# Linear attention with an adapter mixture on one core: epsilon added on VectorE in 16 of 36 steps, logits placed behind the sums of k and v, one batch's sums spread over three steps

## The chip, the core and the metric

The kernel runs on one core of a Trainium2 chip. Its engines each work through their own list of instructions in order: PE (TensorE: matrix products, with PEld for the load of the stationary operand), DVE (VectorE), ACT (ScalarE), POOL (GpSimd) and SP, which here only issues stores. They wait for each other through semaphores. Matrix products land in PSUM, a small memory of eight banks per partition, from where DVE or ACT must move them to SBUF before the bank can be used again. The metric is the device time of one execution in microseconds (us); lower is better.

## What is computed

q, k and v have 8 batches, 8 heads, 576 positions and 64 features. First comes a linear attention whose weights are cos and sin of the position, then a mixture of small adapters over the 4608 rows of 512 features that the attention gives.

```python
r = np.maximum(x, 0.0)
phi(x) = np.concatenate([r * cos_w, r * sin_w], axis=-1)      # for q and for k
kv  = np.einsum('bhsf,bhsd->bhfd', k_p, v)
z   = np.sum(k_p, axis=2)
num = np.einsum('bhsf,bhfd->bhsd', q_p, kv)
den = np.einsum('bhsf,bhf->bhs', q_p, z)[..., None] + 1e-06
x   = num / den
...
logits = x @ w_gate                   # 8 experts, the best 2 are kept
w = softmax of the two kept logits
out = x + sum over the two of w * ((x @ A[e]) @ B[e])
```

The `1e-06` in `den` is the epsilon that the change is about.

## The kernel before

**Tiles.** The 4608 rows are 36 tiles of 128 rows, numbered n from 0 to 35; two batches make nine tiles, of which the middle one (n = 4, 13, 22, 31, called mixed) takes half of its rows from each. The loop `for n in range(NT - 1)` does one tile in each step. The order on every engine is the order in which the program text issues the instructions; no scheduler moves them.

**One step n, in its order.** `evac_x(n-1)` (DVE) copies the transposed x of the tile before from the bank `xz` to `xT`. `normalise(n)` (DVE) takes the reciprocal of the denominators and multiplies, which gives `xt`. `move_q(n+1)` transposes and scales the next tile's q on PE (line 213, from tile 27 on line 201) into two `qd` banks, and ACT moves both to SBUF with the ReLU (line 229). Then come the `logits` of `early_at` (PE, line 300, four products for a tile into the bank `za`), the sums `kv` of `kv_at` (PE, line 180, eight products for one position s, accumulated in the banks `cd`), `gate_a` and `gate_b` of a group of three tiles (DVE, small operations and `zg`), one or two output tiles (`emit`: `delta_x` and `delta_z` on PE into a `qd` bank, or a `cd` bank where the step has no sums, then `evac_o` on ACT and a store), `transp_x(n)` (PE, line 274) and `transp_z` (PE, line 348) of a finished group into `xz`, the DVE, POOL and ACT work on k, the `logits` of `late_at`, and `numden(n+1)` (PE), which gives the numerators and denominators of the next tile in the two banks `nd`.

**What PE's array is set to.** The products of lines 274, 300, 348, 366, 371 and of the full tiles of line 252 use the array as 128 by 128; line 213 as 128 by 64, line 201 as 64 by 64 and line 180 as 64 by 128.

**Epsilon.** In `numden`, a product of a matrix of ones with `eps_hi` (line 247, one for each of the two banks) starts the bank and puts the epsilon where the denominators accumulate; the other products add to it.

**Groups and their due steps.** Tiles are taken in groups g of three. A table built before the loop says in which step the logits of each tile come (`early_at` or `late_at`), `gate_a` of the group, `gate_b` one step later and `transp_z` (`move_at`) one step after that. Group 1 was put one step later than the rule for the others gives. `todo` holds the finished tiles for `emit`.

**k.** For batch b the sums need k scaled by cos and by sin (`kp`), and the ReLU. `relu_k(b, ...)` on DVE applies the ReLU in place in two pieces (line 165: bf16, SBUF to SBUF), in steps 5, 8, 12, 17, 20 and 23 for b = 2 to 7; POOL then scales five to nine positions with two operations each (line 156), and behind the last of them it issues the loads of later batches (line 62). ACT and DVE scale the positions that are left for b = 2 to 5. The sums of batch 2 run in steps 7 and 8, of batch 3 in steps 11 and 12, of batches 4 to 7 in four steps each: 14 to 17, 18 to 21, 23 to 26 and 27 to 30.

Of the kernel before, what the change touches and what calls it, by code (L numbers as in the profile page):

```python
# [8 lines left out]
FP32 = mybir.dt.float32  # L9
# [6 lines left out]
EPS = 1e-6  # L16
# [3 lines left out]
def kernel(ctx, tc, q, k, v, w_gate, A, Bw, out):  # L20
# [163 lines left out]
    def kv_out(b):  # L184
        kv_t[b] = t = p_kv.tile([128, 2, G, W], BF16, name="kvsb")
        for par in range(2):
            src = kvz[par].rearrange("p g u d -> p g (u d)")[:, :, 0:W]
            nc.scalar.copy(t[:, par], src)
# [44 lines left out]
    def move_q(n):  # L233
        transp_q(n)
        evac_q(n, 0)
        evac_q(n, 1)

    def numden(n):
        nd_t[n] = nd = ps.tile([128, 2, 512], FP32, name="nd")
        tok = tokens(n)  # L240
        if mixed(n):
            jobs = [(lo, tok[0][0]), (hi, tok[1][0])]
        else:
            jobs = [(slice(0, 128), tok[0][0])]
        for gg in range(2):
            qpT = qpT_t.pop((n, gg))
            nc.tensor.matmul(out=nd[:, gg, D:4 * W:W], lhsT=ones, rhs=eps_hi, start=True,  # L247
                             stop=False, skip_group_check=True)
            for j in range(4):
                h = 2 * j + gg if quad(n) else gg * 4 + j  # L250
                for pr, b in jobs:
                    nc.tensor.matmul(out=nd[pr, gg, j * W:(j + 1) * W],  # L252
                                     lhsT=qpT[:, j, pr], rhs=kv_t[b][:, h % 2, h // 2, :],
                                     start=False, stop=(j == 3), skip_group_check=True)

    def normalise(n):
        nd = nd_t.pop(n)[:, :, 0:4 * W].rearrange("p g (j x) -> p g j x", x=W)
        rden = p_g.tile([128, H], FP32, name="rden")
        nc.vector.reciprocal(rden, nd[:, :, :, D:W])  # L259
        xt_t[n] = xt = p_x.tile([128, DM], BF16, name="xt")  # L260
        x = xt
        if quad(n):
            x = xt.rearrange("p (g two d) -> p two g d", two=2, d=D)
        else:
            x = xt.rearrange("p (g j d) -> p g j d", g=2, d=D)
        nc.vector.tensor_tensor(  # L266
            out=x, in0=nd[:, :, :, 0:D],
            in1=rden.rearrange("p (g j) -> p g j", g=2).to_broadcast([128, 2, 4, D]),
            op=ALU.mult)
# [153 lines left out]
    for b in range(2, B):  # L423
        first = b // 2 * NS + b % 2 * 4
        at = {2: 5, 3: 8, 4: 12, 5: 17, 6: 20, 7: 23}[b]
        n_pool = {2: 5, 3: 7, 4: 8, 5: 8}.get(b, 9)
        for s0, s1 in ((0, 3), (3, n_pool)):
            put(relu_at, at, (b, s0, s1))
        for s in range(n_pool):
            put(pool_at, at, (b, s))  # L430
        for i in range(2):
            if n_pool <= 7:
                put(dve_at, at, (b, 7, i))
            if n_pool < 9:
                put(act_at, first - 4 + i, (b, 8, i))
            if n_pool == 5:
                put(act_at, first - 3 + i, (b, 6, i))
                put(act_at, first - 2, (b, 5, i))
        order = (7, 0, 1, 2, 3, 4, 8, 6, 5) if n_pool <= 7 else (0, 1, 2, 3, 4, 5, 8, 6, 7)
        if n_pool == 9:  # L440
            order = range(NS)
        for j, s in enumerate(order):

            ahead = (2 if j < 4 else 1) if b < 4 else 4 - min(j // 2, 3)
            put(kv_at, first - ahead, (b, s))


# [2 lines left out]
    prev = 5  # L450
    for g, t in enumerate(groups[:-2]):
        at = max(t[-1] + 1, prev + 1)
        if g == 1:
            at += 1
        for n in t:
            if t[-1] + 1 < at or (n < t[-1] and prev == at - 1):
                put(late_at, at - 1, n)
            else:
                put(early_at, max(n + 1, at - 1), n)
        prev = at + 1  # L460
        put(gate_a_at, at, g)
        put(gate_b_at, at + 1, g)
        put(move_at, at + 2, g)
    put(late_at, NT - 2, NT - 3)

    with tc.manual_schedule():
        for s in range(6):
            make_diag(s)
        wu = qd.tile([128, DM], FP32, name="wu", tag="qd")
        for i in range(24):  # L470
            nc.tensor.matmul(out=wu, lhsT=ones, rhs=wide, start=True, stop=True)  # L471
        for s in range(NS):
            scale_k(0, s, ("act" if s < 7 else "dve", "dve"))
            kv(0, s)
        nc.scalar.activation(warm, halfpi, AF.Sigmoid)
        for s in range(6, NS):
            make_diag(s)
        load_k(1)
        load_v(1)
        load_q(1)  # L480
        load_k(2)
        load_weights()
        load_v(2)
        load_q(2)
        load_k(3)
        load_v(3)
        load_k(4)
        load_q(3)
        load_v(4)
        kv_out(0)  # L490
        transp_q(0)
        evac_q(0, 0, "dve")
        evac_q(0, 1)
        numden(0)

        g10, g11, g12 = range(len(groups) - 3, len(groups))
        todo, held = [], []
        first_loads = persist.tile([1, 8], BF16, name="first_loads")

        def emit(d, own=True, eng="act", add=False):  # L500
            if add:
                delta_add(d, own)
            else:
                delta(d, own)
                evac_o(d, eng)
            if held is None:
                store(d)
            else:
                held.append(d)

        for n in range(NT - 1):
            if n > 0:
                g = move_at.get(n - 1, (None,))[0]
                evac_x(n - 1, g)
                if g is not None:
                    todo += groups[g]
            normalise(n)
            if n != 3:
                move_q(n + 1)
            for t in early_at.get(n, ()):  # L520
                logits(t)
            for b, s in kv_at.get(n, ()):
                kv(b, s)
                if kv_n[b] == NS:
                    kv_out(b)
            if n == 3:
                move_q(n + 1)
            for g in gate_a_at.get(n, ()):
                gate_a(g)
            for g in gate_b_at.get(n, ()):  # L530
                gate_b(g)
            now = todo[:2 if len(todo) > 3 and n not in kv_at else 1]
            del todo[:len(now)]
            for d in now:
                emit(d, n not in kv_at, add=n > 27)
            for g in gate_a_at.get(n, ()):
                gate_sig(g)
            transp_x(n)
            for g in move_at.get(n, ()):
                transp_z(g)  # L540
            for b, s, i in dve_at.get(n, ()):
                scale_k1(b, s, i, "dve")
            for b, s0, s1 in relu_at.get(n, ()):
                relu_k(b, s0, s1)
            for b, s in pool_at.get(n, ()):
                scale_k(b, s)
                if (b, s) == pool_at[n][-1]:
                    if b + 3 < B:
                        load_k(b + 3)
                    if b + 2 < B:  # L550
                        load_q(b + 2)
                    if b + 3 < B:
                        load_v(b + 3)
                    if b + 3 == B - 1:

                        nc.sync.dma_start(out=first_loads, in_=k_b[B - 1][0:1, 0, 0, 0:8])
                        for d in held:
                            store(d)
                        held = None
            for t in late_at.get(n, ()):  # L560
                logits(t)
            numden(n + 1)
            for b, s, i in act_at.get(n, ()):
                scale_k1(b, s, i, "act")


        evac_x(NT - 2)
        normalise(NT - 1)
        transp_z(g10)
        logits(NT - 2)  # L570
        evac_z(g10, [("act", 0, 3)])
        todo += groups[g10]
        for d in todo[:-3]:
            emit(d)
        transp_x(NT - 1)
        gate_a(g11)
        emit(todo[-3])
        gate_sig(g11)
        evac_x(NT - 1)
        logits(NT - 1)  # L580
        gate_b(g11)
        emit(todo[-2])
        gate_a(g12)
        transp_z(g11)
        evac_z(g11, [("act", 0, 2)])
        gate_sig(g12)
        emit(todo[-1])
        gate_b(g12)
        emit(NT - 3)
        transp_z(g12)  # L590
        evac_z(g12, [("dve", 0, 1)])
        emit(NT - 2)
        emit(NT - 1, eng="dve")
# [28 lines left out]
```

## Time and profile before

| | |
|---|---|
| median of 3 runs | 115.53 us (115.42 to 115.57) |
| profiled execution, its own time | 115.39 us |
| span from the first to the last instruction in it | 113.6 us |
| instructions | 5022 |
| granted TensorE clock, mean | 0.995 |
| HBM read and written | 28.85 MB and 9.44 MB |

A row of a group gives the line of the program, the engine, the operation, what it writes and reads with the shape, how often, busy us in total and mean ns of one, and behind the second bar the time that the engine sat idle just before them. A row of the timeline or of the chain of waits gives the start in us from the span's start, the length in us, the engine and what it did; neighbours of one kind are merged, and "x8" is their count. The length of a matrix product reaches from its start to the modelled end of its way through the array, so products overlap, and what one costs in a row of them is the distance between starts.

### The profile page before, as it was taken

The numbers are of one execution on the slowest core, as the hardware profiler recorded it, in microseconds if no ns is written. First come the engines' busy times: TensorE is split into PE (matmuls) and PEld (weight loads), VectorE is DVE, ScalarE is ACT, GpSimd is POOL, SyncE is SP. The second block draws the span as 40 slices with busy tenths as digits, with TensorE's granted clock in tenths as the row PEclk, the third lists the DMA queues.
The fourth block names the chain that finished last, engine by engine and source line by source line (L and its number), as shares of the span: only waits on it lengthen the run. The fifth ranks groups of instructions, "written<-read, shape, count | busy, mean of one in ns | idle before, by whom it ended". The sixth has DMA issues, their size and how long they took to land.

```text
span 113.6 us, 5022 instructions
## 1 busy us (share of the span) xinstructions
PE 99.4 (88%) x2099; PEld 74.2 (65%) x2099; DVE 80.9 (71%) x280; ACT 78.1 (69%) x169; POOL 73.2 (64%) x135
## 2 busy tenths in 40 slices
PE   2999777877898999999999999999999999978710
PEld 1347566766795688777877877777877876754200
DVE  5698488559949958696767886998658478786620
ACT  5077579846995847586876958956777678895720
POOL 5991222238996994999449989989950444984000
PEclk9999999999999999999999999999999999999998
DMA  2999999999999999999999999999988122655892
GB/s 40 383 208 207 207 209 207 208 184 211 204 214 203 206 209 209 208 208 209 207 209 206 211 204 208 260 359 378 380 304 314 52 97 98 175 190 220 291 332 88
DMA packets 19671, 24.77 MB, mean 218 GB/s; under 512 B 2625, under 2 KB 14529, under 8 KB 19649
## 3 DMA queue, kind: packets, MB, share of 16 engines
q0 software_dynamic: 13856, 13.84, 73.2%
q1 hardware_dynamic: 5792, 10.62, 26.4%
q8 instruction: 16, 0.26, 0.9%
q14 instruction: 7, 0.05, 0.1%
HBM read 28.85 MB, written 9.44 MB: 337 GB/s over the span
## 4 chain that ended last, share of the span: by engine, by line
PE 52%; DMA 26%; DVE 11%; POOL 3%; issue 2%; ACT 2%; POOLq 0%; DVEq 0%; ACTq 0%
DMA k<-in_k_dram 14%; DMA v<-in_v_dram 12%; PE cd L180 10%; PE za L300 8%; PE qd L213 7%; PE nd L252 6%; PE xz L274 5%; PE dx L366 4%; DVE xt L266 4%; PE qd L201 3%; PE dx L371 3%; PE xz L348 2%; DVE zg L335 2%; DVE xT L280 2%; ACT qpT L229 1%
## 5 line engine op out<-in xcount | busy, mean ns | idle before, releaser
L229 ACT ACTIVATE qpT<-qd 128x512 bf16<-128x512 f32 x71 | 38.6, 596 | 15.2 <-PE qd L213 11.5
L156 POOL TENSOR_SCALAR kp<-k,cos_tab 128x256 bf16<-128x256 bf16 x46 | 22.5, 490 | 7.2 <-DVE k L165 6.3
L280 DVE COPY xT<-xz 128x512 bf16<-128x512 bf16 (+1 forms) x36 | 17.2, 477 | 13.7 <-PE xz L348 7.5
L266 DVE TENSOR_TENSOR xt<-nd,rden 128x512 bf16<-128x512 f32 x36 | 24.9, 691 | 1.4
L156 POOL TENSOR_SCALAR kp<-k,sin_tab 128x256 bf16<-128x256 bf16 x46 | 21.9, 476 | 0.0
L180 PE MATMUL cd<-v,kp 64*128 64x128 bf16 x576 | 20.1, 217 | 0.8 <-DMA v<-in_v_dram 0.8
L274 PEld LDWEIGHTS <-xt 128*128 128x128 bf16 x144 | 10.8, 115 | 12.0 <-DVE xt L266 7.6
L180 PEld LDWEIGHTS <-kp 64*128 64x128 bf16 x576 | 16.2, 94 | 3.4 <-issue 0.8
L252 PE MATMUL nd<-kvsb,qpT 128*128 128x65 bf16 (+1 forms) x320 | 16.9, 194 | 1.0 <-DVE qpT L231 0.5
L274 PE MATMUL xz<-ident,xt 128*128 128x128 bf16 x144 | 14.4, 222 | 3.6 <-DVE xt L266 3.6
L213 PE MATMUL qd<-diag,q 128*64 128x128 bf16 x432 | 17.2, 222 | 0.0
L391 POOL TENSOR_TENSOR osb<-osb,xt 128x512 f32<-128x512 f32 x9 | 10.2, 1160 | 9.5 <-ACT osb L397 9.0
L397 ACT COPY osb<-dx 128x512 f32<-128x512 f32 x18 | 10.6, 591 | 5.3 <-PE dx L371 5.0
L213 PEld LDWEIGHTS <-q 128*64 128x64 bf16 x432 | 12.9, 109 | 1.5 <-DMA q<-in_q_dram 0.2
L252 PEld LDWEIGHTS <-qpT 128*128 128x128 bf16 (+1 forms) x320 | 12.4, 99 | 1.7 <-ACT qpT L229 0.7
L300 PE MATMUL za<-AW,xT 128*128 128x144 bf16 x140 | 12.2, 227 | 0.6 <-DVE zg L335 0.5
L247 PE MATMUL nd<-eps_hi,ones 128*128 128x4 bf16 x72 | 11.6, 169 | 0.0
L300 PEld LDWEIGHTS <-xT 128*128 128x128 bf16 x144 | 9.1, 98 | 2.8 <-DVE xT L280 0.8
L259 DVE RECIPROCAL rden<-nd 128x8 f32<-128x8 f32 x36 | 7.2, 200 | 4.8 <-PE nd L252 4.8
L397 ACT COPY osb<-cd 128x512 f32<-128x512 f32 x17 | 9.7, 599 | 1.3 <-PE cd L371 1.3
L62 POOL DMA_DIRECT2D v<-in_v_dram x8 | 6.3, 782 | 5.1 <-DMA q<-in_q_dram 4.3
L471 PE MATMUL wu<-wide,ones 128*128 128x512 bf16 x24 | 7.7, 495 | 2.0 <-DVE AW L115 2.0
(73 smaller groups left out, 137.5 us busy)
## 6 DMA issues: line engine op xcount, KB each, us to landing
out_dram<-osb SPq DMA_DIRECT2D x32, 256.0 KB, 3.9
v<-in_v_dram POOLq DMA_DIRECT2D x8, 576.0 KB, 17.2
q<-in_q_dram POOLq DMA_DIRECT2D x8, 576.0 KB, 16.2
k<-in_k_dram POOLq DMA_DIRECT2D x7, 576.0 KB, 15.6
k0f<-in_k_dram SPq DMA_DIRECT2D x1, 1152.0 KB, 5.4
out_dram<-osb SPq DMA_DIRECT2D x8, 128.0 KB, 2.5
AW<-in_moe_A_dram POOLq DMA_DIRECT2D x1, 128.0 KB, 18.1
Ball<-in_moe_B_dram POOLq DMA_DIRECT2D x1, 128.0 KB, 16.5
```

The lines of the kernel that those rows point to most:

```text
L156: nc.gpsimd.tensor_scalar(out=dst, in0=src, scalar1=tab, scalar2=1.0, op0=ALU.mult, op1=ALU.mult)
L180: nc.tensor.matmul(out=kvz[par][:, g], lhsT=kp_t[b][pr, s, g], rhs=v_rhs(b, g, s, pr), start=(first and g == 0), stop=(last and g == G - 1))
L213: nc.tensor.matmul(out=t[cols, j, 2 * gi:2 * gi + 2, :], lhsT=q_b[b][:, 2 * gp + gi, s, :], rhs=diag[:, s, i], start=(j == 0 and gi == 0), ...
L229: nc.scalar.activation(t, src, AF.Relu)
L247: nc.tensor.matmul(out=nd[:, gg, D:4 * W:W], lhsT=ones, rhs=eps_hi, start=True, stop=False, skip_group_check=True)
L252: nc.tensor.matmul(out=nd[pr, gg, j * W:(j + 1) * W], lhsT=qpT[:, j, pr], rhs=kv_t[b][:, h % 2, h // 2, :], start=False, stop=(j == 3), sk ...
L266: nc.vector.tensor_tensor(out=x, in0=nd[:, :, :, 0:D], in1=rden.rearrange("p (g j) -> p g j", g=2).to_broadcast([128, 2, 4, D]), op=ALU.mult)
L274: nc.tensor.transpose(out=xz[:, c * 128:(c + 1) * 128], in_=x[:, c], identity=ident)
L280: nc.vector.tensor_copy(t[:, 0:c], xz[:, 0:c * 128].rearrange("p (c s) -> p c s", c=c))
L300: nc.tensor.matmul(out=za_t[g][:, i, :], lhsT=xT[:, c, :], rhs=AW[:, :, c, :], start=(c == 0 and i == 0), stop=(c == DCH - 1), skip_group_ ...
L391: nc.gpsimd.tensor_tensor(out=t, in0=t, in1=xt_t.pop(n), op=ALU.add)
L397: nc.scalar.copy(t, src)
```

## The change

Four things are edited. `eps_dve(n)` is true in steps after 13 that have sums (n = 14 to 21 and 23 to 30, 16 tiles). For those tiles `numden` leaves out its two products with `eps_hi`; the first product of each bank starts it instead; and `normalise` adds the epsilon with a DVE operation from the bank into a small SBUF tile `den1`, from which the reciprocal is taken. The sums of batch 3 run in steps 10, 11 and 12 (two, three and four positions) and no longer in 11 and 12. Group 1 loses its extra step. And the early logits are issued behind the sums of the step.

```diff
+    def eps_dve(n):
+        return n > 13 and n in kv_at
...
         for gg in range(2):
             qpT = qpT_t.pop((n, gg))
-            nc.tensor.matmul(out=nd[:, gg, D:4 * W:W], lhsT=ones, rhs=eps_hi, start=True,
-                             stop=False, skip_group_check=True)
+            if not eps_dve(n):
+                nc.tensor.matmul(out=nd[:, gg, D:4 * W:W], lhsT=ones, rhs=eps_hi, start=True,
+                                 stop=False, skip_group_check=True)
...
-                                     start=False, stop=(j == 3), skip_group_check=True)
+                                     start=(eps_dve(n) and j == 0), stop=(j == 3),
+                                     skip_group_check=True)
...
-        nc.vector.reciprocal(rden, nd[:, :, :, D:W])
+        den = nd[:, :, :, D:W]
+        if eps_dve(n):
+            den1 = p_g.tile([128, 2, 4, 1], FP32, name="den1")
+            nc.vector.tensor_scalar(out=den1, in0=den, scalar1=EPS, scalar2=None, op0=ALU.add)
+            den = den1
+        nc.vector.reciprocal(rden, den)
...
-            ahead = (2 if j < 4 else 1) if b < 4 else 4 - min(j // 2, 3)
+            if b == 2:
+                ahead = 2 if j < 4 else 1
+            elif b == 3:
+                ahead = 3 if j < 2 else 2 if j < 5 else 1
+            else:
+                ahead = 4 - min(j // 2, 3)
             put(kv_at, first - ahead, (b, s))
...
         at = max(t[-1] + 1, prev + 1)
-        if g == 1:
-            at += 1
...
-            for t in early_at.get(n, ()):
-                logits(t)
             for b, s in kv_at.get(n, ()):
                 kv(b, s)
                 if kv_n[b] == NS:
                     kv_out(b)
+            for t in early_at.get(n, ()):
+                logits(t)
```

What follows from the tables: the logits of group 1 move from step 8 to step 7, those of group 2 from 10 to 9, of tiles 9 and 10 from 12 to 11 (tile 11 stays in 12, now early), and those of tiles 12 and 13 stay in step 14 but are early there. The gates of groups 1, 2 and 3 come one step earlier, later groups keep theirs. Step 13 emits two output tiles where it emitted one, each step from 14 to 30 emits the tile that came one step later before, and step 31 emits one in place of two. Early logits and sums then meet in 13 steps: 12, 14, 15, 17, 18, 20, 21, 23, 24, 26, 27, 29 and 30; before it was in 11 of them, all but 12 and 14.

## The prediction

> **What bounds the kernel now.** I read the page first.
>
> ```profile
> PE 99.4 (88%) x2099; PEld 74.2 (65%) x2099; DVE 80.9 (71%) x280; ACT 78.1 (69%) x169; POOL 73.2 (64%) x135
> PE 52%; DMA 26%; DVE 11%; POOL 3%; issue 2%; ACT 2%; POOLq 0%; DVEq 0%; ACTq 0%
> ```
>
> PE is busiest and holds half of the chain that ended last. The chain in order of time and the table of stretches say where.
>
> ```profile
> 18.67 15.62 DMA k<-in_k_dram
> ...
> 45.86 0.75 PE za L300 x12
> ...
> 56.93 0.57 PE qd L213 x16
> 57.50 0.61 PE za L300 x8
> 58.10 0.78 PE cd L180 x24
> 58.88 0.32 PE dx L366
> ...
> 72.13 0.22 PE cd L371
> ```
>
> ```profile
> 48.70:78.00 29.30, 29.19 (x601) 22.82 (x599) 23.63 (x73) 21.60 (x47) 25.42 (x54) 1.00 1.19 236
> ```
>
> Up to 34.3 us the loads set the pace (the load of k in the first row is batch 3's). Behind that the chain is nearly all PE, which is busy for 29.19 of 29.30 us in steps 14 to 24. But POOL has 25.42 in the same stretch, the second number. So I looked at how POOL and DVE meet there, since the chain of waits gives only the last waiter.
>
> ```profile
> 54.48 0.77 POOL L62 DMA_DIRECT2D v<-in_v_dram  x1
> 57.24 0.69 DVE L266 TENSOR_TENSOR xt<-nd,rden 128x512 bf16<-128x512 f32 x1
> 57.85 0.75 DVE L165 TENSOR_SCALAR k<-k 128x768 bf16<-128x768 bf16 x2
> 58.30 0.64 POOL L156 TENSOR_SCALAR kp<-k,cos_tab 128x256 bf16<-128x256 bf16 x1 [3.06 <-DVE k L165]
> ...
> 66.81 0.63 POOL L156 TENSOR_SCALAR kp<-k,cos_tab 128x256 bf16<-128x256 bf16 x1 [0.33 <-issue]
> ...
> 73.79 2.05 DVE L165 TENSOR_SCALAR k<-k 128x768 bf16<-128x768 bf16 x2
> 74.68 0.48 POOL L156 TENSOR_SCALAR kp<-k,sin_tab 128x256 bf16<-128x256 bf16 x1
> 75.65 0.53 POOL L156 TENSOR_SCALAR kp<-k,cos_tab 128x256 bf16<-128x256 bf16 x1 [0.49 <-PE xz L348]
> 75.76 0.61 DVE L280 COPY xT<-xz 128x896 bf16<-128x896 bf16 x1
> 76.29 0.19 DVE L259 RECIPROCAL rden<-nd 128x8 f32<-128x8 f32 x1
> 76.52 0.69 DVE L266 TENSOR_TENSOR xt<-nd,rden 128x512 bf16<-128x512 f32 x1
> ```
>
> ```profile
> L165 DVE TENSOR_SCALAR k<-k x12: 273/486/1584, 26.5 to 75.3; 128x768 bf16<-128x768 bf16 x6, 128x1280 bf16<-128x1280 bf16 x2, 128x1536 bf16<-128x1536 bf16 x2, 128x512 bf16<-128x512 bf16 x1
> ```
>
> This is a second chain, hidden under PE's. POOL is idle until `relu_k(5)` at 57.85 (step 17), then scales batch 5, issues a load, and runs batch 6 from 66.81 without a pause. `relu_k(7)` starts at 73.79 in step 23 and takes 2.05 us for its two pieces, where the pair at 57.85 took 0.75. One piece took 1584 ns. It ends just after POOL's last operation on batch 6 (74.68 + 0.48 = 75.16): the DVE operation is held until POOL pauses. Behind it stand `evac_x(23)` at 75.76, the reciprocal at 76.29 and `xt` of tile 24 at 76.52. So in step 24 DVE is on time with POOL, and POOL's time is that of `relu_k(5)` plus a fixed length.
>
> **The change part by part.**
>
> *Epsilon off PE.*
>
> ```profile
> L247 PE MATMUL nd<-eps_hi,ones 128*128 128x4 bf16 x72 | 11.6, 169 | 0.0
> ```
>
> ```profile
> 76.42 0.42 PE L300 MATMUL za<-AW,xT 128*128 128x144 bf16 x4
> 77.78 0.39 PE L274 MATMUL xz<-ident,xt 128*128 128x128 bf16 x4
> 78.00 0.17 PE L247 MATMUL nd<-eps_hi,ones 128*128 128x4 bf16 x1
> 78.03 0.28 PE L252 MATMUL nd<-kvsb,qpT 128*128 128x65 bf16 x4
> ```
>
> 169 ns is the way through the array; the slot is 78.03 − 78.00 = 0.03 us. 32 products go: 32 × 0.03 = 0.96 us of PE, 0.06 for each of 16 tiles.
>
> *Epsilon on DVE.* No row shows this add. The nearest ones:
>
> ```profile
> L259 DVE RECIPROCAL rden<-nd 128x8 f32<-128x8 f32 x36 | 7.2, 200 | 4.8 <-PE nd L252 4.8
> L314 DVE TENSOR_TENSOR mask<-za,m 128x24 f32<-128x24 f32 x11 | 1.9, 173 | 0.0
> L311 DVE TENSOR_REDUCE nm<-m 128x3 f32<-128x6 f32 x11 | 1.7, 159 | 0.4
> ```
>
> The first two read a bank, the third SBUF, and all write a few values. I take 0.20 us (the row with its very shape), between 0.16 (the third row) and 0.23 (76.52 − 76.29, from one reciprocal to what waits for it); an instruction more cannot win time on DVE. It lies between `nd` and `xt`, and `transp_x` waits for `xt`. In a step with sums PE has sums, logits or an output tile to do meanwhile, so it costs nothing where PE is behind; where DVE is behind, it costs 0.20.
>
> *Logits behind the sums.* In the chain 12 logits products before `nd` take 0.75, that is 0.0625 each; 8 of them before the sums take 0.61, not 0.50. The 0.1 is a change of the array's setting from 128 by 128 to 64 by 128. Before: line 213, logits, sums, output: three changes. After: line 213, sums, logits, output: two, because logits and output have one setting. 0.10 in each of the 11 steps which had both: 1.1 us. On DVE `gate_a` waits longer for its logits, by the length of the sums (0.55 to 0.78 less the 0.10); what is late next is `evac_x` behind it, by a tenth or two where I follow it, and PE's next need of that `xT` is a step away.
>
> *Batch 3 in three steps, group 1 one step earlier, one more output tile before step 14.* From 34.3 to 49 us.
>
> ```profile
> 39.32 0.91 PE L300 MATMUL za<-AW,xT 128*128 128x144 bf16 x12 [0.26 <-DVE zg L335]
> 47.83 0.38 PE L371 MATMUL cd<-Ball,xT 128*128 128x512 bf16 x1
> 48.26 0.41 PE L274 MATMUL xz<-ident,xt 128*128 128x128 bf16 x4
> 50.66 0.39 PE L274 MATMUL xz<-ident,xt 128*128 128x128 bf16 x4
> 51.07 0.66 PE L300 MATMUL za<-AW,xT 128*128 128x144 bf16 x8
> ```
>
> ```profile
> 45.11 0.75 DVE L165 TENSOR_SCALAR k<-k 128x768 bf16<-128x768 bf16 x2
> 45.57 0.64 POOL L156 TENSOR_SCALAR kp<-k,cos_tab 128x256 bf16<-128x256 bf16 x1 [1.69 <-DVE k L165]
> ```
>
> The wait for `zg` at 39.32 goes from group 2's logits in step 10 to the same logits in step 9: there `za` is freed by `zg` of group 1, one `gate_b` (0.7) behind `xt`, so it stays. Two waits go. `transp_x(13)` comes 0.43 after the product before it, not 0.22 as usual (48.26 − 47.83): the second output tile of step 13 fills those 0.21. The logits of tiles 12 and 13 come 0.41 after the transposes, not 0.22: 0.19, and behind the sums they find `xT` ready. A third step with sums adds a change of setting, 0.1 to 0.15. Sum: 0.27 won, with bounds −0.4 (DVE leads) and +0.6 (the wait at 39.32 goes too). The extra output tile costs two products of 0.22 before step 24, 0.43. It comes back in step 31, where it buys nothing, since `transp_x(31)` waits for `xt` there. In step 12 `gate_a(3)` now waits for logits behind the sums, and `relu_k(4)` stands behind it: tile 11's logits end near 45.7 as I follow PE, DVE sees them 0.2 later, `gate_a` has six small operations at 0.1 each: about 46.6, an estimate, where it was 45.11. POOL then ends batch 4 and its three loads near 56.7 (before, 54.48 + 0.77 = 55.25), still ahead of `relu_k(5)`. The loads of k, q and v of batches 7, 6 and 7 are issued 1.4 us later; they are used 20 us on.
>
> *The sum.* Start of step 17 on PE: +0.43 (tile) − 0.24 (epsilon of tiles 14 to 17) − 0.10 (step 15) − 0.27 = −0.18. `relu_k(5)` follows with one add on its path: 57.85 − 0.18 + 0.20 = 57.87, as before. So POOL's second chain stands where it stood, `relu_k(7)` is held until 75.2 again, though PE reaches it over a microsecond earlier, and `evac_x(23)` comes at 75.8. From there: reciprocal formerly 0.53 later (76.29 − 75.76), now the add takes this place; reciprocal 0.20 on; `xt` 0.23 on (76.52 − 76.29), 0.69 long: 75.78 + 0.53 + 0.20 + 0.23 + 0.69 = 77.43, and `transp_x(24)` 0.05 later at 77.5 where it was 77.78. Only 0.3 us of all that steps 14 to 24 save is left. The logits of tile 23, 76.42 before, cannot come earlier either; but the sums run ahead of them and no longer behind, which is where the 0.3 come from.
>
> Behind step 24: four steps with both, 4 × 0.10 = 0.40. Of six epsilons that of tile 25 counts, 0.06. The rest go into another wait:
>
> ```profile
> 80.18 0.59 ACT L397 COPY osb<-dx 128x512 f32<-128x512 f32 x1 [0.19 <-PE dx L371]
> ```
>
> ```profile
> 80.66 0.15 PE qd L201 x2
> ```
>
> From tile 27 on line 201 writes both `qd` banks at once, one of which holds the output tile until ACT has moved it (80.18 + 0.59 = 80.77); PE goes on only then. Removing work between the output tile and line 201 moves nothing. Together 0.3 + 0.40 + 0.06 = 0.8. The profiled execution has 115.39 (span 113.6, 1.8 around it), so 114.6; the median of the runs lies 0.14 above it. I say 114.6, its range 114.2 to 115.0: add and regrouping at their bounds.
>
> The Trainium skill, SBUF — State Buffer, section "Who interferes with whom", says that `tensor_scalar` in its two-port modes locks GpSimd out or is locked out, and that whoever issues first has the ports for the whole instruction. By that alone `relu_k(7)` would get them after one POOL operation of 0.48; the trace shows it waiting through three. By the page the time would be that of the first rival.
>
> **The rivals.**
>
> *POOL does not hold `relu_k(7)`* or `relu_k(5)` comes earlier. All terms count: 7 × 0.10 + 10 × 0.06 + 0.27 − 0.43 = 1.14 up to step 24, plus 0.46: 1.6, so 113.8. Against it: the 1584 ns.
>
> *`relu_k(5)` late, slower.* Break-even is 0.8 behind my 57.87. If DVE leads from step 12 on (`gate_a(3)` behind the sums, then `relu_k(4)`, then `evac_x(12)`), the adds of tiles 14 to 17 count four times, not once (+0.6), and the regrouping loses 0.4 in place of winning 0.27 (+0.67): 1.27 late, 0.5 us beyond break-even, 115.9. For it: DVE's 23.63 of 29.30 and one operation more in each step. Against it stand DVE's own waits for PE in that stretch, such as the 0.56 here, which would absorb most of it:
>
> ```profile
> 52.06 0.21 DVE L259 RECIPROCAL rden<-nd 128x8 f32<-128x8 f32 x1 [0.56 <-PE nd L252]
> ```
>
> *The new reciprocal reads SBUF and is held by POOL as `relu_k` is.* POOL works on batch 4 until about 54.4, so step 14's reciprocal at 49.8 would wait 4.6: 119 or more. Against it: only line 165's form is seen held. The Trainium skill, in the same section of SBUF — State Buffer, names copies, casts and `tensor_scalar` as the forms that can take the shared ports, not the reciprocal; no run here shows it.
>
> *The front eats the gain:* `relu_k(5)` 0.3 to 0.7 late, 114.9 to 115.3, or close to 115.5.
>
> **How the numbers follow.** Forecast 0.48, no hold 0.13, small gain 0.15, no change 0.07, slower by late `relu_k(5)` 0.13, held reciprocal 0.04. 0.2% (0.23 us) is about what a measurement here tells from nothing. Faster 0.48 + 0.13 + 0.15 = 0.76, same 0.07, slower 0.17. The range 113.7 to 115.8 takes in the first rival and the small gains, and leaves out most of the slower ones.
>
> **What would show it.** Right: `relu_k(5)` within 0.3 of 57.85; first piece of `relu_k(7)` over 1.6 us long, starting near 73; `transp_x(24)` near 77.5; PE idle over half a microsecond in step 24; 0.5 won between there and tile 31. Wrong: `relu_k(7)` short, `relu_k(5)` behind 58.7, or reciprocals longer than 0.25.

## The result and the profile after

| | before | after |
|---|---|---|
| median (lowest to highest of 6 runs) | 115.55 us (115.42 to 115.83) | 114.53 us (114.27 to 114.66) |
| ratio, 95% interval | | 0.9909 [0.9894, 0.9924] |
| profiled execution: own time, span | 115.39, 113.6 us | 114.54, 112.8 us |

The change wins 1.02 us between the medians and 0.85 us between the two profiled executions. One execution (115.80 us, of the kernel without epsilon below) is over 1.5% longer than the fastest of its kernel and is left out of its median as slow. From the page of the kernel after, the busy times and the shares of the chain that ended last:

```profile
PE 96.1 (85%) x2050; PEld 74.1 (66%) x2068; DVE 83.7 (74%) x296; ACT 78.2 (69%) x169; POOL 72.3 (64%) x134
PE 40%; DMA 28%; DVE 15%; issue 4%; POOL 4%; ACT 4%; POOLq 0%; DVEq 0%; ACTq 0%
```

PE lost 3.3 us of busy time, but the kernel only one: PE's share of the chain fell from 52% to 40%, and DVE's rose from 11% to 15%. The chain of waits in order of time (start, length, engine, what it did) shows where DVE came in; before, the same stretch was nearly all PE:

```profile
69.91 0.25 PE nd L257 x8
...
72.72 0.21 DVE rden L270
72.96 0.06 DVE xt L277
...
73.57 2.36 DVE k L165 x2
75.93 0.53 DVE xT L291
76.46 0.09 DVE den L268
76.57 0.21 DVE rden L270
76.81 0.70 DVE xt L277
77.55 0.41 PE xz L285 x4
```

The two pieces of `relu_k(7)` (line 165) now stand on the chain with 2.36 us. Around them, on the timeline of DVE, POOL and PE of the kernel after (start, length, line, operation; in brackets the engine's idle time and what ended it):

```profile
58.15 0.75 DVE L165 TENSOR_SCALAR k<-k 128x768 bf16<-128x768 bf16 x2
...
74.77 0.49 POOL L156 TENSOR_SCALAR kp<-k,sin_tab 128x256 bf16<-128x256 bf16 x1
...
75.85 0.61 DVE L291 COPY xT<-xz 128x896 bf16<-128x896 bf16 x1
76.38 0.15 DVE L268 TENSOR_SCALAR den<-nd 128x8 f32<-128x8 f32 x1
76.52 0.42 PE L311 MATMUL za<-AW,xT 128*128 128x144 bf16 x4 [0.16 <-DVE xT L291]
76.57 0.20 DVE L270 RECIPROCAL rden<-den 128x8 f32<-128x8 f32 x1
76.81 0.69 DVE L277 TENSOR_TENSOR xt<-nd,rden 128x512 bf16<-128x512 f32 x1
77.55 0.41 PE L285 MATMUL xz<-ident,xt 128*128 128x128 bf16 x4 [0.40 <-DVE xt L277]
```

`relu_k(5)` stands 0.30 later than before (58.15, was 57.85), so POOL's last operation on batch 6 ends 0.10 later (74.77 + 0.49 = 75.26, was 75.16). The first piece of `relu_k(7)` starts 0.22 earlier (73.57, was 73.79) and, as one group of line 165 shows, takes 1899 ns where it took 1584:

```profile
L165 DVE TENSOR_SCALAR k<-k x12: 275/453/1899, 26.6 to 75.4; 128x768 bf16<-128x768 bf16 x6, 128x1280 bf16<-128x1280 bf16 x2, 128x1536 bf16<-128x1536 bf16 x2, 128x512 bf16<-128x512 bf16 x1
```

It ends at 73.57 + 1.90 = 75.47, again 0.2 behind POOL. PE, which was busy for 29.19 of 29.30 us up to here before, now waits in step 24: 0.16 + 0.40 = 0.56 us.

The start of `transp_x(n)` in each profile, less the start of the same transposes before (negative is earlier), shows in which steps the time is won. All columns but the first are such differences; the kernels to the right are the experiments below.

| step n | before, us | after | epsilon alone | logits alone | regrouping alone | epsilon + logits | after, `relu_k(5)` earlier | after, POOL waits for itself |
|---|---|---|---|---|---|---|---|---|
| 9 | 36.83 | +0.11 | −0.01 | +0.18 | +0.11 | +0.05 | +0.11 | +0.09 |
| 14 | 50.66 | +0.88 | −0.05 | +0.19 | +0.94 | 0.00 | +0.88 | +0.86 |
| 17 | 59.25 | 0.00 | +0.10 | −0.02 | +0.32 | −0.07 | 0.00 | −0.03 |
| 23 | 74.97 | −0.53 | −0.05 | −0.45 | +0.32 | −0.60 | −0.53 | −0.56 |
| 24 | 77.78 | −0.22 | +0.11 | −0.66 | +0.31 | −0.25 | −0.74 | −0.83 |
| 30 | 93.09 | −0.80 | +0.09 | −1.22 | +0.31 | −0.82 | −1.32 | −1.40 |
| 35 | 103.68 | −0.86 | +0.09 | −1.20 | +0.25 | −0.82 | −1.37 | −1.45 |

(The +0.88 of step 14 belongs to the regrouping, which has +0.94 alone.) The row of step 9 is the scatter from one execution to the next: epsilon alone, logits alone and the pair of them issue the same instructions as the kernel before up to step 12, and stand at −0.01, +0.18 and +0.05. An execution keeps this difference up to step 17 (step 17 less step 9 is −0.11 or −0.12 in all three columns with the whole change), so what a part does up to there is read less its column's step 9. Between steps 17 and 23 the kernel wins 0.53, in the one step 24 it gives 0.31 back, and from there to step 30 it wins 0.58.

### The profile page after: what moved, and what is told of

Its sections match the earlier page's. It is cut to its first block, busy times and chain, and to the rows that moved or that the text cites. A ratio compares the mean times of both kernels' runs of the same rounds, so it can differ in the third digit from the quotient of the medians.

```text
span 112.8 us, 4956 instructions
## 1 busy us (share of the span) xinstructions
PE 96.1 (85%) x2050; PEld 74.1 (66%) x2068; DVE 83.7 (74%) x296; ACT 78.2 (69%) x169; POOL 72.3 (64%) x134
## 4 chain that ended last, share of the span: by engine, by line
PE 40%; DMA 28%; DVE 15%; issue 4%; POOL 4%; ACT 4%; POOLq 0%; DVEq 0%; ACTq 0%
DMA k<-in_k_dram 14%; DMA v<-in_v_dram 12%; PE cd L180 9%; PE za L311 7%; PE qd L213 6%; PE xz L285 5%; PE nd L257 4%; DVE xt L277 4%; PE dx L377 3%; DVE k L165 3%; DVE xT L291 2%; DVE zg L346 2%; ACT osb L408 2%; PE qd L201 2%; DMA out_dram<-osb 2%
## 5 line engine op out<-in xcount | busy, mean ns | idle before, releaser
L402 POOL TENSOR_TENSOR osb<-osb,xt 128x512 f32<-128x512 f32 x8 | 9.2, 1160 | 9.6 <-ACT osb L408 8.0
L408 ACT COPY osb<-dx 128x512 f32<-128x512 f32 x19 | 11.2, 588 | 5.9 <-remote 2.1
L408 ACT COPY osb<-cd 128x512 f32<-128x512 f32 x16 | 9.1, 597 | 1.3 <-PE cd L382 1.3
L62 POOL DMA_DIRECT2D q<-in_q_dram x8 | 6.1, 763 | 3.6 <-DMA k<-in_k_dram 3.6
L62 POOL DMA_DIRECT2D k<-in_k_dram x7 | 5.4, 771 | 3.9 <-DMA k<-in_k_dram 2.2
```

The costliest lines, as they stand in the source:

```text
L62: eng.dma_start(out=t, in_=rows(dram, b))
L402: nc.gpsimd.tensor_tensor(out=t, in0=t, in1=xt_t.pop(n), op=ALU.add)
L408: nc.scalar.copy(t, src)
```

## The experiments

Every kernel was timed against the kernel before on the same chip. The kernel before had medians of 115.41 to 115.55 in these sessions, so a tenth between two kernels' medians means nothing. "First piece" is that of `relu_k(7)`, from its profile.

| kernel | median, us | ratio, 95% | first piece, ns |
|---|---|---|---|
| epsilon alone | 115.52 | 1.001 [1.0001, 1.0018] | 1494 |
| logits alone | 114.18 | 0.9894 [0.9881, 0.9908] | 1741 |
| regrouping alone | 115.60 | 1.0021 [1.0005, 1.0036] | 1572 |
| epsilon + logits | 114.55 | 0.9919 [0.9906, 0.9932] | 1945 |
| after, without epsilon | 114.18 | 0.9897 [0.9880, 0.9914] | 1748 |
| after, `relu_k(7)` one step later | 114.21 | 0.9897 [0.9884, 0.9910] | 360 |
| after, `relu_k(5)` one step earlier | 113.98 | 0.9870 [0.9856, 0.9884] | 1382 |
| the same, without epsilon | 114.19 | 0.9896 [0.9883, 0.9909] | 1332 |
| after, one product on POOL repeated | 114.00 | 0.9872 [0.9859, 0.9884] | 585 |
| after, an extra operation behind batch 6 | 114.95 | 0.9954 [0.9942, 0.9966] | 2022 |
| after, the extra operation early in batch 6 | 114.82 | 0.9957 [0.9942, 0.9972] | 2024 |
| the same, waiting for POOL itself | 113.94 | 0.9865 [0.9848, 0.9881] | 659 |

**Each part by itself.** Three kernels take one of the parts of the change each: the new place of the early logits; `eps_dve` with the add; or the steps of batch 3 and group 1 with the due steps that follow.

> The kernel before with the early logits behind the sums alone. Theory: relu_k(5) about 0.1 us earlier; in step 24 the 0.55 us of sums run while the logits wait for xT of tile 23, so transp_x(24) comes at 77.2 to 77.3 (before 77.78), then four changes of the array's setting fewer. Gain 0.8 to 1.0 us, ratio 0.991 to 0.993: as much as the whole change. Rival (only the 11 changes of setting count, spread evenly): 0.4 us by step 24 and 1.0 us at the end, but with transp_x(24) no earlier than 77.4.

> The kernel before with the epsilon edit alone. Theory (POOL holds relu_k(7) in step 23, so DVE is on POOL's time in step 24): relu_k(5) stays within 0.1 us of 57.85, evac_x(23) near 75.8, and because the logits of tile 23 still run ahead of the sums, transp_x(24) stays at 77.7 to 77.8; behind step 24 only tile 25's epsilon counts. Gain 0 to 0.2 us, ratio 0.998 to 1.000. Rival (every term counts where it stands): 14 tiles of 0.06 us, gain 0.7 to 0.9 us, ratio 0.992 to 0.994.

> The kernel before with batch 3's sums in three steps and group 1 one step earlier, no other edit. Theory: relu_k(5) comes 0.3 to 0.6 us later (one more output tile, one more stage of sums before it), POOL's batches 5 and 6 and the hold of relu_k(7) move by the same, and nothing gives it back: 0.3 to 0.6 us slower, ratio 1.003 to 1.005. Rival (my prediction's sum for this part, 0.27 won and 0.43 for the output tile that step 31 gives back): within 0.2 us of before.

The placing of the logits alone gives 1.2 us, more than the 0.8 to 1.0 expected and more than the whole change. Step by step, its transposes come 0.10 to 0.17 earlier in each of the steps 15, 17, 18, 20, 21, 23, 26, 27, 29 and 30, which have both sums and early logits. Where it comes from shows in PE's products of one such step, 18, before:

```profile
60.60 0.42 PE L300 MATMUL za<-AW,xT 128*128 128x144 bf16 x4
60.96 0.62 PE L180 MATMUL cd<-v,kp 64*128 64x128 bf16 x16
61.51 0.39 PE L366 MATMUL dx<-xt,ident 128*128 128x512 bf16 x1
```

and with the logits behind the sums:

```profile
60.58 0.62 PE L180 MATMUL cd<-v,kp 64*128 64x128 bf16 x16
61.13 0.42 PE L300 MATMUL za<-AW,xT 128*128 128x144 bf16 x4
61.40 0.38 PE L366 MATMUL dx<-xt,ident 128*128 128x512 bf16 x1
```

The sums take 0.55 from their start to the next in both. The four logits products take 0.36 where products of another setting follow them (64 by 128) and 0.27 where the next has the same one: about 0.10 for one change of setting. The kernel meets the hold too, but PE has just enough to do meanwhile. DVE and PE of that kernel:

```profile
73.45 2.20 DVE L165 TENSOR_SCALAR k<-k 128x768 bf16<-128x768 bf16 x2
75.58 0.61 DVE L280 COPY xT<-xz 128x896 bf16<-128x896 bf16 x1
76.11 0.19 DVE L259 RECIPROCAL rden<-nd 128x8 f32<-128x8 f32 x1
76.42 0.42 PE L300 MATMUL za<-AW,xT 128*128 128x144 bf16 x4
77.11 0.39 PE L274 MATMUL xz<-ident,xt 128*128 128x128 bf16 x4
```

No bracket stands behind the products of 76.42 and 77.11: PE came to both as their input was ready. In the kernel after, `relu_k(5)` is 0.21 later (58.15 against 57.94), so `evac_x(23)` follows at 75.85, and the add puts the reciprocal one place further back, 76.57 against 76.11. That is the 0.56 of idle PE.

Epsilon alone wins nothing, though 32 products go and 0 to 0.2 us were expected; `relu_k(5)` comes at 58.23, and not within 0.1 of 57.85. Two rows of PE in that kernel show where the gain goes.

```profile
51.26 0.41 PE L311 MATMUL za<-AW,xT 128*128 128x144 bf16 x4 [0.26 <-DVE zg L346]
...
76.54 0.42 PE L311 MATMUL za<-AW,xT 128*128 128x144 bf16 x4 [0.25 <-DVE xT L291]
```

What PE saves it waits for: 0.26 on `zg`, since DVE has a longer list in step 14, and 0.25 on `xT` behind the held `relu_k(7)`. The regrouping alone leaves step 17 at +0.32, of which 0.11 stands at step 9 already: it wins 0.22 against the 0.43 of its extra output tile, and the kernel is 0.2 slower, less than the 0.3 to 0.6 expected.

**Two parts together, and the whole without epsilon.**

> The kernel before with the epsilon edit and the logits behind the sums, batch 3 and group 1 as before. Theory: the add is paid on DVE's way twice, in step 14 (zg of group 3 comes 0.2 us later and the late logits of tiles 12 and 13 wait for it) and in step 24 (xt of tile 24 behind the held relu_k(7)), and PE's 0.06 for each tile before step 24 ends in the hold. 0.1 to 0.3 us slower than logits alone: 114.3 to 114.5 us, ratio 0.990 to 0.992. Rival (the epsilon edit saves PE 0.5 us once the logits no longer stand in the way): 113.6 to 113.9 us, ratio 0.984 to 0.987.

> The changed kernel with the epsilon back on PE in all tiles (logits behind the sums and the regrouping stay). Theory: the regrouping makes relu_k(5) late by 0.2 to 0.3 us as it did alone, POOL's chain and the hold move with it, and without the add xt of tile 24 comes 0.2 us sooner behind the hold: between the changed kernel and logits alone, 114.3 to 114.5 us, ratio 0.990 to 0.992. Rival (the epsilon edit pays inside the whole change): slower than the changed kernel by 0.3 us or more, 114.8, ratio 0.995.

Epsilon and logits together take as long as the whole change (114.55 and 114.53): the regrouping gives back its tile and no more in that company, as it takes away the wait for `zg` at 51.26. Without epsilon the whole change takes 114.18, with it 114.53 (`relu_k(5)` comes at 57.89 there, and not 0.2 to 0.3 late as the theory had it); and logits alone 114.18, with epsilon 114.55. Epsilon costs 0.3 to 0.4 here. The intervals of the first pair overlap and those of the second just touch; the traces carry it: step 24 stands at −0.71 without epsilon and at −0.22 with it.

**`relu_k(7)` behind the hold.** The due step of `relu_k(7)` is put from 23 to 24, where POOL has run out of batch 6:

```diff
-        at = {2: 5, 3: 8, 4: 12, 5: 17, 6: 20, 7: 23}[b]
+        at = {2: 5, 3: 8, 4: 12, 5: 17, 6: 20, 7: 24}[b]
```

> The changed kernel with relu_k(7) and POOL's batch 7 in step 24 and not in 23. POOL has ended batch 6 by then. Theory: no piece of relu_k(7) is longer than 0.6 us, PE does not idle in step 24, the lead of 0.53 us that transp_x(23) has is kept and grows: 0.3 to 0.5 us faster than the changed kernel, 114.0 to 114.2 us; ratio to the kernel before 0.987 to 0.989. Rival (the hold is hidden, PE is the bound): same as the changed kernel, ratio 0.990 to 0.992.

The first piece takes 360 ns and step 24 stands at −0.61, but step 25 falls back to −0.15. DVE and PE of that kernel:

```profile
77.58 0.83 DVE L165 TENSOR_SCALAR k<-k 128x768 bf16<-128x768 bf16 x2
78.33 0.41 DVE L291 COPY xT<-xz 128x512 bf16<-128x512 bf16 x1
...
79.84 0.36 PE L285 MATMUL xz<-ident,xt 128*128 128x128 bf16 x3 [0.32 <-DVE xt L277]
```

The pair no longer waits, but its 0.83 us now stand between `gate_a` and `evac_x(24)`, and PE waits 0.32 for the `xt` behind them. Still, the time is 0.3 less than that of the kernel after. (This profile, of 114.49 us, has a granted clock of 0.938.)

**`relu_k(5)` earlier.** If POOL's second chain starts at `relu_k(5)`, one step earlier there should bring the end of batch 6 forward.

```diff
-        at = {2: 5, 3: 8, 4: 12, 5: 17, 6: 20, 7: 23}[b]
+        at = {2: 5, 3: 8, 4: 12, 5: 16, 6: 20, 7: 23}[b]
```

> The changed kernel with relu_k(5) and POOL's batch 5 in step 16 and not in 17. POOL idles for 1.75 us before relu_k(5), so batches 5 and 6 move 1.5 to 2 us earlier and POOL has ended batch 6 when relu_k(7) comes in step 23. Theory: no piece of relu_k(7) over 0.9 us, transp_x(24) at 77.1 to 77.2 (before 77.78, changed kernel 77.55) and 0.3 to 0.5 us faster than the changed kernel: 114.0 to 114.2, ratio 0.987 to 0.989. Rival (the hold costs nothing, DVE or ACT bound step 24 in another way): the same as the changed kernel, 114.5, ratio 0.991.

> The changed kernel without its epsilon edit and with relu_k(5) one step earlier. Theory: with the hold cut short by the earlier relu_k(5) the add costs little in step 24 (the changed kernel with relu_k(5) earlier took 113.98), so the edit's matmuls are a small gain or nothing, and without it the time is 113.9 to 114.2. Rival (the add costs in every step in which it stands, not in step 24 alone): 113.65 to 113.8, by the same 0.3 as between the whole change and the change without epsilon.

DVE and POOL of the first of the two:

```profile
56.57 0.84 DVE L165 TENSOR_SCALAR k<-k 128x768 bf16<-128x768 bf16 x2
...
65.87 0.82 DVE L165 TENSOR_SCALAR k<-k 128x768 bf16<-128x768 bf16 x2
66.39 0.64 POOL L156 TENSOR_SCALAR kp<-k,cos_tab 128x256 bf16<-128x256 bf16 x1 [1.09 <-issue]
...
73.57 1.84 DVE L165 TENSOR_SCALAR k<-k 128x768 bf16<-128x768 bf16 x2
74.26 0.47 POOL L156 TENSOR_SCALAR kp<-k,sin_tab 128x256 bf16<-128x256 bf16 x1
...
75.33 0.61 DVE L291 COPY xT<-xz 128x896 bf16<-128x896 bf16 x1
```

`relu_k(5)` is 1.58 us earlier than in the kernel after, but POOL's end of batch 6 only 0.53 (74.26 + 0.47 = 74.73, was 75.26). Between the two batches POOL now stands idle, until `relu_k(6)` of step 20 at 65.87. So POOL has not ended batch 6 when `relu_k(7)` comes, and the first piece still takes 1382 ns, where at most 900 were expected. By the same half microsecond `evac_x(23)` comes earlier (75.33, was 75.85), step 24 keeps its lead (−0.74), and the time is 113.98, less than before and after the change. Here epsilon is no longer a loss: without it the time is 114.19, and the intervals just touch. Of the 0.38 between the two traces at the end, 0.10 lies in steps 17 to 23; 0.24 lies in one gap of PE in step 28 of the second kernel which no wait explains, so the size of epsilon's gain stays open.

**Is it POOL's run that holds `relu_k(7)`?** The last chain of tests lengthens it. First, the product of sin on position 0 of batch 6 is done twice:

```diff
             for b, s in pool_at.get(n, ()):
                 scale_k(b, s)
+                if (b, s) == (6, 0):
+                    scale_k1(b, s, 1, "pool")
```

> The changed kernel with one of POOL's 18 operations on batch 6 done twice (0.45 us from start to start). Theory: POOL's chain is the bound at step 24, so the hold gets longer by 0.45 and so does the time: evac_x(23) 0.45 later, 114.9 to 115.0 us, ratio 0.994 to 0.996. Rival (POOL has slack, which its 64% of the span suggests): no change from the changed kernel, ratio 0.991.

This went against the theory: 114.00, half a microsecond less, where 0.45 more was expected. The first piece took 585 ns and POOL went on with batch 6. Either the hold is not what it seemed, or the edit did more than lengthen the run: the second product overwrites what the first wrote, so it waits on POOL's own semaphore. Three more kernels separate the two. Two of them let the extra operation write a tile that nothing reads, behind position 8 or behind position 0:

```diff
+                if (b, s) == (6, 8):        # (6, 0) in the second kernel
+                    scr = p_kp.tile([128, G, D], BF16, name="scr", bufs=1)
+                    nc.gpsimd.tensor_scalar(out=scr, in0=k_b[b][:, :, s, :], scalar1=sin_tab[:, s:s + 1],
+                                            scalar2=1.0, op0=ALU.mult, op1=ALU.mult)
```

> The changed kernel with one more operation on POOL at the end of its batch 6, from k to a tile that nothing reads. Theory (relu_k(7) is held until POOL's run of batch 6 ends): the run ends 0.45 us later, so the first piece of relu_k(7) grows from 1899 ns to 2.3 us or more, evac_x(23) goes from 75.85 to 76.3, step 24 loses 0.45, and the time is 114.9 to 115.0. Rival (the hold is let go at some boundary between two operations of POOL, and the end of the run is chance): first piece at most 1.9 us, time 114.0 to 114.6.

> The changed kernel with the same extra operation behind the first pair of batch 6, so that the run's length is as in the run before, but every later operation is shifted by one place and, unlike in the kernel with the repeated multiplication, none waits on POOL's own semaphore. If the repeated operation's own wait let DVE in, there is none here: first piece 2.3 us, 114.9 to 115.0. If the shift by one operation did it (DVE gets in where POOL's instructions stand differently in their stream): first piece near 0.6 us and 114.0, as before with the repeated one.

Both are 0.3 to 0.4 slower (114.95 and 114.82), near the time that the theory asks for, but not in the way it asks. The first piece takes 2.02 us and not 2.3 or more. The rest of the loss is in the second piece, which now meets POOL at work (0.75 us for 0.54). In the third kernel the extra operation at position 0 takes as its input what POOL has just written, and so waits for it:

```diff
-                    nc.gpsimd.tensor_scalar(out=scr, in0=k_b[b][:, :, s, :], scalar1=sin_tab[:, s:s + 1],
+                    nc.gpsimd.tensor_scalar(out=scr, in0=kp_t[b][:, s, :, 1, :], scalar1=sin_tab[:, s:s + 1],
```

> As the run with the extra operation behind the first pair of batch 6 that nothing reads (114.82, first piece of relu_k(7) 2024 ns), but its input is the product that POOL has just written, so that it waits on POOL's own semaphore, as the repeated multiplication did; length, place and number of operations are the same. If that wait is what let DVE in 6 us later: first piece near 0.6 us, evac_x(23) near 74.9, 114.0. If something else in the kernel with the repeated multiplication did it: first piece 2.0 us, 114.8 to 114.95.

The timelines of POOL and DVE, without that wait:

```profile
73.33 0.47 POOL L156 TENSOR_SCALAR kp<-k,sin_tab 128x256 bf16<-128x256 bf16 x1
73.55 2.70 DVE L165 TENSOR_SCALAR k<-k 128x768 bf16<-128x768 bf16 x2
73.79 0.47 POOL L156 TENSOR_SCALAR kp<-k,cos_tab 128x256 bf16<-128x256 bf16 x1
...
75.14 0.69 POOL L156 TENSOR_SCALAR kp<-k,sin_tab 128x256 bf16<-128x256 bf16 x1
```

and with it:

```profile
73.50 0.48 POOL L156 TENSOR_SCALAR kp<-k,sin_tab 128x256 bf16<-128x256 bf16 x1
73.54 1.41 DVE L165 TENSOR_SCALAR k<-k 128x768 bf16<-128x768 bf16 x2
73.96 0.58 POOL L156 TENSOR_SCALAR kp<-k,cos_tab 128x256 bf16<-128x256 bf16 x1
74.52 0.78 POOL L156 TENSOR_SCALAR kp<-k,sin_tab 128x256 bf16<-128x256 bf16 x1
75.00 0.62 DVE L291 COPY xT<-xz 128x896 bf16<-128x896 bf16 x1
75.27 0.48 POOL L156 TENSOR_SCALAR kp<-k,cos_tab 128x256 bf16<-128x256 bf16 x1
```

Without the wait POOL's operations run at full speed past DVE (0.47 each) until the run's last, which is slowed to 0.69, and `relu_k(7)` takes 2.70 us. Its first piece ends at 73.55 + 2.02 = 75.57, a quarter of a microsecond ahead of the run's end (75.14 + 0.69 = 75.83), where in the kernel after it ended 0.2 behind it. With the wait DVE gets in at the next boundary between two operations of POOL; POOL's two are then slowed to 0.58 and 0.78, and the pair is done after 1.41 us, in the middle of POOL's run. The time is 113.94, the least of all. Where in a POOL operation the request falls is not the reason: in the kernel with epsilon alone it came 0.11 us after the start of one and was held, in the one with the repeated product it came 0.11 us after the start of one and was let in.

So the theory stands in part. `relu_k(7)` is passed over at two or three boundaries between POOL's operations, and no semaphore of POOL's run explains it: it waits for the same three semaphores in the traces of both kernels above, and in the second one it is through in the middle of the run. What ends the hold is not shown. In all eleven kernels that have it, before and after among them, DVE gets in, by the end of the first piece less its own 0.35 us, at about the end of the run's 18th operation, which is the run's last in nine of them but not in the two with an operation more. And the hold does not belong to every run: in the two kernels with a wait of POOL on itself, at 68.0 and so 5.5 us ahead of the request, it is gone. How, stays open. That wait also spares POOL's first operation on batch 7 its own wait on the same semaphore, so that the kernels differ in two waits, and it wasn't tried which of them counts.

## Why the prediction was right

The time (114.53 for a predicted 114.6) and the mechanism were right: a DVE operation held by POOL decides step 24, and what PE saves before it is lost there. Some sizes were wrong in both directions, and that the step was hit to 0.05 us is partly luck.

*The hold.* The forecast had PE arriving early at a step that DVE and POOL decide: `transp_x(24)` at 77.5, measured 77.55; `relu_k(5)` within 0.3 of 57.85, measured 58.15, just inside; first piece over 1.6 us, measured 1.90; PE idle over half a microsecond in step 24, measured 0.56. Starting POOL's work earlier (`relu_k(5)` in step 16) gained 0.55, lengthening the run lost 0.3 to 0.4, and the two kernels in which DVE gets in at once gained 0.5 and 0.6.

*The luck.* The prediction took POOL's time in step 24 as that of `relu_k(5)` plus a fixed length. The length is not fixed: from `relu_k(5)` to the end of batch 6 it is 17.31 us before (57.85 to 75.16), 17.11 after (58.15 to 75.26) and 18.16 with `relu_k(5)` in step 16 (56.57 to 74.73). POOL also needs `relu_k(6)` for batch 6, and so it idled before that batch: 0.33 in the kernel before (the bracket at 66.81), 1.09 at 66.39 above; in the kernel after it did not. This took up most of the 0.28 by which `relu_k(5)` came later than the 57.87 of the sum, and `evac_x(23)` came at 75.85, forecast at 75.78.

*Logits behind the sums.* 0.10 per step was right, and so was the place: 0.36 against 0.27 for the four logits products of step 18. The 0.17 of steps 27 and 30 was not forecast and is not explained here. This is the part that carries the gain: 1.2 us alone.

*Epsilon off PE.* This term was mis-sized. Its 0.06 per tile was credited with 0.24 up to the start of step 17 (the first product of line 213 there). Less step 9's difference, the whole change stands at −0.05 there and at +0.10 without epsilon, so epsilon won 0.15; alone it lost 0.07, since DVE is late for `zg` in step 14. Beside the logits it won 0.10 from step 17 to 23 (−0.53 for the pair, −0.43 for the logits alone), where five tiles at 0.06 would give 0.30. The slot itself is 0.05 per tile: from the first product into `nd` to line 213 PE takes 0.39 with the ones and 0.34 without (64.32 to 64.71 with the logits alone, 64.22 to 64.56 for the pair). But a PE that comes sooner to line 213 can find its second bank still holding the output tile of the step before. In the pair:

```profile
61.93 0.59 ACT L408 COPY osb<-dx 128x512 f32<-128x512 f32 x1 [0.41 <-PE za L311]
62.29 0.69 PE L213 MATMUL qd<-diag,q 128*64 128x128 bf16 x16
```

and with the logits alone:

```profile
62.44 0.64 PE L213 MATMUL qd<-diag,q 128*64 128x128 bf16 x16
```

ACT's copy ends at 61.93 + 0.59 = 62.52, the ninth product of line 213, the first into that bank, waits for ACT and starts at 62.57, the line takes 0.05 longer, and the slot is lost. The prediction had this wait for line 201 only.

*The add.* Predicted at 0.20, bounds 0.16 to 0.23; no row had shown it. It does now, as do the two forms of the reciprocal:

```profile
L268 DVE TENSOR_SCALAR den<-nd 128x8 f32<-128x8 f32 x16 | 2.5, 155 | 0.0
L270 DVE RECIPROCAL rden<-den 128x8 f32<-128x8 f32 x16 | 3.3, 203 | 0.6
L270 DVE RECIPROCAL rden<-nd 128x8 f32<-128x8 f32 x20 | 4.1, 203 | 4.2 <-PE nd L257 4.1
```

The add takes 155 ns, and 0.19 from its start to the reciprocal's (76.38 to 76.57). That the reciprocal from SBUF might be held by POOL, a rival at 4%, falls: 203 ns from either memory, under a working POOL as well.

*Regrouping.* 0.27 was to be won against an extra tile of 0.43, that is +0.16 up to step 17. Alone it came to +0.21 (+0.32 less the 0.11 of step 9), and beside the other two parts to nothing (−0.05 for the whole, −0.04 for the pair), as it takes away the wait for `zg`. So PE starts step 17 at 56.91, was 56.86: +0.05, where −0.18 was forecast. Of that difference 0.11 is this execution's, 0.09 epsilon's and the small rest the regrouping's, and `relu_k(5)` followed at 58.15 and not at 57.87.

*Behind step 24.* 0.46 was predicted, 0.58 measured from step 24 to 30. Logits alone win 0.56 there, so the four steps give 0.14 each on average and not 0.10, and epsilon almost nothing, as the wait for ACT's copy had suggested.

*The rivals.* The first one, no hold, was priced at 113.8. It didn't happen, but the kernel in which POOL waits for itself comes near that case, with 113.94. The late `relu_k(5)` came by 0.3 and not by the 0.8 of the break-even point. The rule of the Trainium skill, SBUF — State Buffer, section "Who interferes with whom", by which the lock lasts one instruction, describes what was seen in the two kernels with POOL's own wait (let in at the next boundary, 0.42 us after the request in the trace above); in all the others that asked during the run the measurement says otherwise, with first pieces of 1332 to 2024 ns.

## What to carry to other kernels

When one engine is busy nearly all the time, ask which other pair of engines is on time with it, and follow that chain from its last free point: work taken off the busy engine is won only up to the next place where the two meet. A small operation added to the second chain can cost more there than the instructions that it replaces, and the same edit can turn to a gain once that chain has slack, so test the parts of a change by themselves and together. Order products by the array's setting: moving the logits behind the sums won 1.2 us with no work removed.

## What was not expected of the hardware

A bf16 `tensor_scalar` on DVE from SBUF to SBUF, 0.35 us by itself, took up to 2.02 us while POOL ran `tensor_scalar` operations back to back: it was passed over at two or three of the boundaries between them. In the two kernels in which POOL waited on its own semaphore some 12 operations earlier, the same instruction got in at the first boundary (0.59 and 0.66 us), at the price of two slower POOL operations (0.58 and 0.78 us for 0.48). In the two kernels with an extra operation and the hold, the first piece ended a quarter of a microsecond ahead of the end of POOL's last operation of the run, which took 0.69 us for 0.47; in the kernel after it ended 0.2 us behind that end. What makes POOL give way is open.
